# Fewer warm-up matmuls, an earlier load of the beta row, and x matmuls moved ahead of kv groups at the start of an attention and SwiGLU-like kernel

## The chip, the cores and the metric

One core of one Trainium2 chip. The metric is the device time of one execution in microseconds (us). The kernel before took 282.32 us, median of 3 runs (282.05, 282.32 and 292.75). The span of the profiled execution, 280.1 us, is what the engines show between first and last instruction. "Granted clock" is the mean clock of the TensorE in an execution as the profile records it, 1.0 being full.

## The reference

Shapes: q, k, v are 8 batches x 8 heads x 576 rows x 64. The feed-forward has 512 inputs, 2048 hidden units, 512 outputs, on 4608 rows.

```python
q_s = exp(q - max(q, -1));  q_s = q_s / (sum(q_s, -1) + 1e-9)      # softmax over head_dim
k_s = exp(k - max(k, 2));   k_s = k_s / (sum(k_s, 2) + 1e-9)       # softmax over the rows
kv  = einsum('bhsd,bhse->bhde', k_s, v)
x   = einsum('bhsd,bhde->bhse', q_s, kv)   # heads side by side: 4608 x 512
h   = x @ w_in
out = (h * (1 / (1 + exp(-beta * h)))) @ w_out
```

## The kernel before

The program is scheduled by hand: each engine gets its instructions in the order of the source. Batch 0 begins on empty buffers. Its heads are handled in four pairs ("groups"): q is exponentiated, normalised and transposed (`tpe`), k is exponentiated (`kz_exp`), v cast (`vz_cast`), both multiplied into a small kv matrix (`kvz_mm`), which DVE normalises into `kvp` (`kvz_norm`), and kv times q gives the input of the feed-forward (`xpe`, copied by `xev`). Then `hpe` starts the feed-forward's matmuls.

```python
def warm(n, tag):                       # matmuls on zeros, result unused
    t = ps.tile([P, 512], F32, tag=bank(tag), bufs=1, name=...)
    for _ in range(n):
        nc.tensor.matmul(t[:], xT[2][:, 0, 0:P], xT[2][:, 0, :])

def xpe(c, j, tag):
    t = x_ps[c, j] = ps.tile([P, MAIN], F32, tag=bank(tag), bufs=1, name=...)
    nc.tensor.matmul(t[:], kvp[:, c, j, :], qsT[c][:, :, j, :])

def beta_pe(tag):                       # beta's row turned onto partitions
    tb = ps.tile([P, 512], F32, tag=bank(tag), bufs=1, name="tb")
    nc.tensor.transpose(tb[:, 0 : NJ // 2], beta_r[:, 0 : 2 * P : 2], ident8[:])
    nc.tensor.transpose(tb[:, NJ // 2 : NJ], beta_r[:, 1 : 2 * P : 2], ident8[:])
# ... (cut: the other helpers)
load_q(0, 4, [0]); load_q(0, 4, [1, 2, 3], nc.scalar)
load_kv(k_st, k, 0, "k_st", whole=True)
# v groups 0, 1, 2; beta row; v group 3; then w_in block 0 in four, w_in block 1 in two, w_out, ...
# ... (cut: memsets)
warm(18, tag="b0")
# ... (cut: exps and sums of q)
warm(10, tag="acc2")
tpe(0, 2, "acc3")
# ... warm(1), tpe(0, 1), warm(1)
kvz_mm(0, 0, "acc3", 1)                 # kv 0
tpe(0, 3, "acc1")
kvz_mm(0, 1, "acc2", 1)                 # kv 1
beta_pe("acc0")
kvz_mm(0, 2, "acc3", 1)                 # kv 2
xpe(0, 0, "acc1")                       # x 0
kvz_mm(0, 3, "acc2", 1)                 # kv 3
xpe(0, 1, "acc0"); xpe(0, 2, "b3")      # x 1, x 2
hpe(0, 0, [0], "b0"); hpe(0, 1, [0], "b1")
xpe(0, 3, "acc3")                       # x 3
# ... (cut: the rest; the calls for ACT, DVE and POOL stand between these lines)
```

The softmax here doesn't subtract the row's maximum and nothing guards it: scores larger than these inputs give would overflow.

## Time and profile before

| | before |
|---|---|
| median of 3 runs | 282.32 us |
| span of the profile | 280.1 us |
| TensorE (PE) busy | 275.6 us, 98% |
| first v group landed | 10.11 us |
| kv 1 begins | 12.21 us |
| h matmuls without large gaps from | 15.17 us |
| first matmul into the output accumulators | 21.89 us |

The lines behind this table are in the prediction. To read them: an engine's row lists start, length, engine, source line, operation, output and input, and in square brackets how long the engine was idle just before and what ended that. PEld is the loading of weights, which runs beside PE; ACT, DVE and POOL are the scalar, vector and GpSimd engines, SP the one that issues most transfers. A matmul's printed length is its modelled end (0.38 us); in a dense stream of 512 columns one starts every 0.217 us.

### The profile page before, as it was taken

To read this page: it belongs to the slowest core of one execution; us is meant where nothing else is said; L and a number is where in the kernel's file an instruction comes from. 1 tells how busy PE (TensorE), PEld (TensorE's weight loads), DVE (VectorE), ACT (ScalarE), POOL (GpSimd) and SP (SyncE) were. 2 spreads that over 40 slices of the span, in tenths; PEclk is the share of its full clock that TensorE was granted. 3 is DMA by queue.
4 is the path that set the end of the run, shared out by engine and by line. 5 is a ranking of instruction groups with operands and counts; after the bars stand their busy time and mean duration, and the time that the engine had idled before them with its cause. 6 is when DMAs were issued, how large, how long until landed. Compare 5 with 4: busy or idle time off the path is not lost.

```text
span 280.1 us, 4485 instructions
## 1 busy us (share of the span) xinstructions
PE 275.6 (98%) x1744; PEld 128.7 (46%) x1744; DVE 175.3 (63%) x285; ACT 162.6 (58%) x248; POOL 38.3 (14%) x58
## 2 busy tenths in 40 slices
PE   8999999999999999999999999999999999999995
PEld 3544454444444444444444444444444544444544
DVE  3964786994478456945595549553864596354362
ACT  3767885948486447744684559444733574454451
POOL 1555237133030003000300030000000000000000
DMA  7999999999981992199418951641144034005004
GB/s 247 391 378 392 386 389 324 315 278 154 320 284 43 252 289 75 71 237 278 125 78 218 274 147 75 132 95 75 75 86 142 0 152 75 0 0 152 0 0 150
DMA packets 55316, 50.09 MB, mean 179 GB/s; under 512 B 26616, under 2 KB 47488, under 8 KB 55296
## 3 DMA queue, kind: packets, MB, share of 16 engines
q1 hardware_dynamic: 54368, 48.97, 60.4%
q10 hardware_dynamic: 928, 0.85, 0.9%
q8 instruction: 13, 0.21, 0.3%
q14 instruction: 7, 0.06, 0.1%
HBM read 36.71 MB, written 9.44 MB: 165 GB/s over the span
## 4 chain that ended last, share of the span: by engine, by line
PE 95%; DMA 3%; POOL 1%; SPq 0%; issue 0%; ACT 0%
PE h L404 44%; PE acc L453 44%; DMA v_st<-in_v_dram 3%; PE kv L342 2%; PE x L373 1%; PE acc L445 1%; PE kv L317 1%; PE x L389 1%; POOL va L174 1%; PE tp L298 0%; SPq L132 0%; SPq L109 0%; ACT o L172 0%; PE x L364 0%; PE tb L565 0%
## 5 line engine op out<-in xcount | busy, mean ns | idle before, releaser
L418 DVE SCALAR_TENSOR_TENSOR g<-th,h 128x512 bf16<-128x512 bf16 x144 | 96.2, 682 | 79.3 <-ACT th L414 79.0
L414 ACT ACTIVATE th<-h,beta_t 128x512 bf16<-128x512 f32 x144 | 97.8, 686 | 81.0 <-PE h L404 80.3
L404 PE MATMUL h<-xT,w_in_b 128*128 128x512 bf16 x576 | 143.2, 379 | 0.0
L453 PE MATMUL acc<-w_out_b,g 128*128 128x512 bf16 x560 | 141.0, 379 | 0.0
L404 PEld LDWEIGHTS <-w_in_b 128*128 128x128 bf16 x576 | 55.9, 98 | 66.3 <-ACT w_in_b L172 0.7
L453 PEld LDWEIGHTS <-g 128*128 128x128 bf16 x560 | 53.8, 98 | 66.0 <-issue 2.5
L174 POOL CAST va<-v_st 128x2048 bf16<-128x2048 f32 (+2 forms) x14 | 17.1, 1231 | 115.7 <-DMA v_st<-in_v_dram 115.7
L262 DVE TENSOR_REDUCE rq<-eq 128x16 f32<-128x1024 bf16 (+1 forms) x20 | 22.1, 1105 | 5.7 <-ACT eq L251 5.3
L268 DVE TENSOR_TENSOR eq<-eq,rq 128x1024 bf16<-128x1024 bf16 (+1 forms) x20 | 22.9, 1151 | 0.1
L172 ACT CAST xT<-x 128x512 bf16<-128x512 f32 x18 | 9.9, 588 | 17.0 <-PE x L373 14.9
L251 ACT ACTIVATE eq<-q_st 128x1024 bf16<-128x1024 f32 (+1 forms) x18 | 16.9, 955 | 3.5 <-DMA q_st<-in_q_dram 3.5
L174 DVE COPY o<-acc 128x512 f32<-128x512 f32 (+2 forms) x20 | 12.6, 642 | 3.6 <-PE acc L453 3.4
L172 ACT COPY o<-acc 128x512 f32<-128x512 f32 (+1 forms) x18 | 9.5, 570 | 8.4 <-PE acc L453 4.6
L174 DVE CAST xT<-x 128x512 bf16<-128x512 f32 x18 | 11.5, 683 | 2.6 <-PE x L373 1.8
L193 ACT ACTIVATE ek<-k_st 128x1024 bf16<-128x1024 f32 x12 | 12.6, 1051 | 0.0
L532 PE MATMUL warm<-xT 128*128 128x512 bf16 x30 | 9.4, 469 | 1.2 <-DVE xT L613 1.2
L174 POOL CAST w_in_b<-w_in 128x512 bf16<-128x512 f32 (+1 forms) x9 | 5.9, 660 | 6.1 <-DMA w_in<-in_moe_w_in_dram 6.0
L174 POOL CAST w_out_b<-w_out 128x1024 bf16<-128x1024 f32 x5 | 5.2, 1041 | 6.3 <-DMA w_out<-in_moe_w_out_dram 6.3
L532 PEld LDWEIGHTS <-xT 128*128 128x128 bf16 x30 | 3.4, 117 | 5.7 <-issue 3.0
L186 ACT ACTIVATE ek<-k_st 128x576 bf16<-128x576 f32 x8 | 5.0, 674 | 1.2 <-DMA k_st<-in_k_dram 1.0
L263 DVE RECIPROCAL rq<-rq 128x16 f32<-128x16 f32 (+1 forms) x20 | 4.9, 243 | 0.7
L342 PEld LDWEIGHTS <-ek 128*64 128x64 bf16 x192 | 4.1, 111 | 2.5 <-issue 2.5
(48 smaller groups left out, 83.7 us busy)
## 6 DMA issues: line engine op xcount, KB each, us to landing
out_dram<-o SPq DMA_DIRECT2D x14, 512.0 KB, 3.4
q_st<-in_q_dram SPq DMA_DIRECT2D x25, 256.0 KB, 4.3
k_st<-in_k_dram SPq DMA_DIRECT2D x6, 1024.0 KB, 9.7
v_st<-in_v_dram SPq DMA_DIRECT2D x6, 1024.0 KB, 11.7
w_in<-in_moe_w_in_dram SPq DMA_DIRECT2D x6, 512.0 KB, 9.8
v_st<-in_v_dram SPq DMA_DIRECT2D x8, 288.0 KB, 8.6
w_out<-in_moe_w_out_dram SPq DMA_DIRECT2D x4, 512.0 KB, 9.0
w_out<-in_moe_w_out_dram SPq DMA_DIRECT2D x2, 1024.0 KB, 9.8
```

The source lines that it names most:

```text
L172: eng.copy(dst, src)
L174: eng.tensor_copy(dst, src)
L193: nc.scalar.activation(ek[b][:, :, h, :].rearrange("p i h d -> p h i d"), k_st[b][:, h, 0 : R * D].rearrange("p h (i d) -> p h i d", i=R), ...
L251: nc.scalar.activation(eq[b][:, :, s * m : (s + 1) * m, :].rearrange("p i h d -> p h i d"), q_st[b][:, s * m : (s + 1) * m, :].rearrange(" ...
L262: nc.vector.tensor_reduce(rq[b][:, 0, :, h], eq[b][:, :, h, :], axis=AX.X, op=ALU.add)
L268: eng.tensor_tensor(eq[b][:, :, h, :], eq[b][:, :, h, :], rq[b][:, 1, :, h].unsqueeze(3).to_broadcast((P, R, m, D)), ALU.mult,)
L342: nc.tensor.matmul(t[r * D : (r + 1) * D, j, :], ek[b][:, i, hd, :] if i < R else ekt[(b // 2) % 2][:, ds(hd * D, D)], va[b][:, i, hd, :] ...
L404: nc.tensor.matmul(h[:], w_unit(j, kt), x_of(c)[:, kt, :], start=(kt == 0), stop=(kt == KT - 1),)
L414: nc.scalar.activation(th[:], h_of[c, j][:], ACTF.Tanh, scale=beta_t[:, j : j + 1])
L418: nc.vector.scalar_tensor_tensor(out=g[:], in0=th_of.pop((c, j))[:], scalar=1.0, in1=h_of[c, j][:], op0=ALU.add, op1=ALU.mult)
L453: nc.tensor.matmul(acc[st][:], g[:, ds(st * P, P)], w_out_b[:, j, :], start=(j == 0), stop=(j == NJ - 1),)
L532: nc.tensor.matmul(t[:], xT[2][:, 0, 0:P], xT[2][:, 0, :])
```

## The change

Its intent: less PE time spent on warm-ups that may hold the first transposes; the beta transposes out of the path behind kv 1; x groups as early as their kv is normalised.

```diff
     load_kv(k_st, k, 0, "k_st", whole=True)
+    nc.sync.dma_start(beta_r[:], moe_beta.rearrange("(hh q) -> hh q", q=2 * P))
     load_kv(v_st, v, 0, "v_st", [0])
     load_kv(v_st, v, 0, "v_st", [1])
     load_kv(v_st, v, 0, "v_st", [2])
-    nc.sync.dma_start(beta_r[:], moe_beta.rearrange("(hh q) -> hh q", q=2 * P))
 (cut)
-    warm(18, tag="b0")
+    warm(14, tag="b0")
 (cut)
-    warm(10, tag="acc2")
+    warm(8, tag="acc2")
 (cut)
-    warm(1, tag="acc1")
+    beta_pe("acc0")
     kvz_mm(0, 0, "acc3", 1)
 (cut)
-    beta_pe("acc0")
     kvz_norm(0, 1)
+    xpe(0, 0, "b3")
     kvz_mm(0, 2, "acc3", 1)
 (cut)
-    xpe(0, 0, "acc1")
     kvz_norm(0, 2)
+    xpe(0, 1, "acc0")
     kvz_mm(0, 3, "acc2", 1)
 (cut)
-    xpe(0, 1, "acc0")
     kvz_norm(0, 3)
-    xpe(0, 2, "b3")
+    xpe(0, 2, "acc1")
```

## The prediction

> **What bounds the kernel now.** I read the page first, for the engine that is full and the chain that ends last.
>
> ```profile
> PE 275.6 (98%) x1744; PEld 128.7 (46%) x1744; DVE 175.3 (63%) x285; ACT 162.6 (58%) x248; POOL 38.3 (14%) x58
> ...
> PE   8999999999999999999999999999999999999995
> ...
> DMA  7999999999981992199418951641144034005004
> ...
> PE 95%; DMA 3%; POOL 1%; SPq 0%; issue 0%; ACT 0%
> ```
>
> The TensorE (PE) is the bound for 265 of 280.1 us. Only the first slices are not yet so: the second row begins with 8, and the DMA row is full for the first twelve slices. All parts of the change lie in the first 15 us, so the question is how much earlier, if at all, the dense matmuls can begin. Next came the chain of waits in the window from 0 to 18 us (start, length, what):
>
> ```profile
> 1.74 8.37 DMA v_st<-in_v_dram
> 10.11 0.06 issue
> 10.16 2.00 POOL va L174 x2
> 12.16 0.04 issue
> 12.21 0.48 PE kv L317 x18
> 12.68 0.21 PE tb L565
> 12.89 0.12 PE tb L566
> 13.02 0.41 PE kv L317 x18
> 13.42 0.32 PE x L389
> 13.74 0.41 PE kv L317 x18
> 14.15 0.54 PE x L389 x2
> ```
>
> Up to 12.21 the first v group's landing and two POOL casts set the time, not PE. From there PE works without a gap worth naming. The beta transposes (tb) take 0.33 us there, between kv 1 and kv 2, and one x matmul between two kv groups takes 0.32. Then I read the timeline by engine, in narrow stretches, for what lets each later instruction go:
>
> ```profile
> 13.78 0.58 ACT L172 CAST xT<-x 128x512 bf16<-128x512 f32 x1 [0.56 <-PE x L389]
> 14.51 0.58 ACT L172 CAST xT<-x 128x512 bf16<-128x512 f32 x1
> 14.99 0.62 ACT L172 CAST w_in_b<-w_in 128x512 bf16<-128x512 f32 x1
> 14.90 0.10 PEld L389 LDWEIGHTS <-kvp 128*128 128x128 bf16 x1 [0.28 <-DVE kvp L332]
> 15.66 0.12 PEld L404 LDWEIGHTS <-w_in_b 128*128 128x128 bf16 x2 [0.39 <-ACT w_in_b L172]
> 19.01 0.62 ACT L172 CAST w_in_b<-w_in 128x512 bf16<-128x512 f32 x1
> 19.05 0.61 POOL L174 CAST w_in_b<-w_in 128x512 bf16<-128x512 f32 x1 [0.75 <-DMA w_in<-in_moe_w_in_dram]
> 19.68 0.14 PEld L404 LDWEIGHTS <-w_in_b 128*128 128x128 bf16 x2 [0.29 <-ACT w_in_b L172]
> ```
>
> The last three rows are the ones to see. The second half of w_in block 1 (issued 11.62, 7.4 us to landing) lands at 19.0; its ACT cast ends at 19.63; the weight load that needs it goes at 19.68. From 15.17 to 19.73 PE starts a matmul every 0.217 us and loses 0.23 us in two places: 0.065 at 15.67 (that ACT cast of block 0) and 0.165 at 19.30 (a PSUM bank that the DVE product frees at 19.25). So even with the whole front earlier, the matmul at 19.73 cannot go before about 19.68. That is an anchor set by DMA.
>
> Third, who fills the DMA: over the stretch from 2 to 21 us the windows give a DMA share of 0.83 to 1.10 in every microsecond, 251 to 420 GB/s. There is no empty slot for an earlier issue to fill.
>
> **What the Trainium skill says.** "TensorE: Matmul & The Clock Gate", Part 1, holds that the array runs at 1.2 GHz until about 3.4 us of activity in a free-running window, that it goes back after an idle window of that length, and gives 426.7 and 215.7 ns per 512-column matmul. The trace agrees with the first half: the warm-up weight loads lie 0.43 us apart from 1.59 to 5.81, then matmuls start every 0.217 us. The granted clock column shows 1.00 there too, so it does not show this gate; the spacing does. No fall back is seen. Part 4 adds that transposes do not count as busy in the same way; this trace cannot test it. "DMA: Bandwidth & Descriptors", "Queues, rings and completion order", says that each SDMA engine consumes one issuer's descriptors in ring order. The trace agrees: the four v groups, issued at 1.74 to 3.75, land 8.4 to 8.8 us later, behind k, which lands at 9.3. "SBUF — State Buffer" has a shared DVE and POOL port held for a whole instruction; here the same 128x576 POOL cast took 0.92, 1.13 and 0.66 us, the longest beside a DVE product, which fits. The change does not move those two against each other.
>
> **The change part by part.**
>
> Fewer warm-ups, 18 to 14. Eleven run cold (1.19 + 11 x 0.43 = 5.9); the four removed are fast ones, 4 x 0.217 = 0.87 us. The first transpose moves from 7.32 to about 6.5 (its DVE product ends at 6.30). It gains nothing: its copy on ACT waits in order behind the exps, until 7.81, and after that copy ACT waits for k (1.02 us idle until 9.40). Second group, 10 to 8: 2 x 0.217 = 0.43 us. The next transpose waits at 10.07 for its DVE product (9.31 + 0.64 = 9.95). The eight end about 8.45 instead of 9.7, so PE idles 1.6 us instead of 0.37. Value on the path: 0.
>
> Beta. The row's load is 8 KB and costs SP 0.38 us to issue. Moved ahead of v, it makes v groups 0 to 2 issue 0.42 us later, but their descriptors queue behind k until about 9.3 us, so landing moves only by the 8 KB: at 390 GB/s 0.02 us, on the engines that carry it perhaps 0.04 (an estimate). Beta lands right after k, near 9.4. Its two transposes take the place of the single warm-up before kv 0 (0.31 us), around 10.9, and cost 0.33: nothing, as kv 0 waits for the POOL cast until 11.1. It takes 0.33 us out of the stretch behind kv 1.
>
> x groups earlier. x 0 needs its kvp normalised (DVE 12.30 + 0.23 = 12.53), so it fits straight after kv 1 at 12.62 and fills 0.32, exactly the slot beta left. kv 2 stays at 12.95 (its POOL cast ends 12.76). x 1 now stands before kv 3 and needs the norm of kv 1, which ends at 13.39: it goes at 13.45 rather than 13.36. So kv 3 starts at 13.76 instead of 13.67, and everything behind it in the DVE chain (norm of kv 3, x 3) shifts by +0.09: x 3 at 15.05. Before it, one x matmul fewer lies behind kv 3 (0.22 us), but x 3 already waited 0.28 us for DVE, so that only widens the wait.
>
> What is won: ACT can copy x 0 at 13.23 instead of 13.78 and x 1 at 13.87 instead of 14.51, and ends the w_in cast at 15.10 instead of 15.61. The 0.065 us stall at 15.67 goes.
>
> Sum: +0.09 (x 1 waits for its norm) + 0.04 (8 KB ahead of v) - 0.065 (stall gone) = +0.07 us at 15.7. At 19.73 it is held by the anchor from below (gain at most 0.05), and by carried shift from above. Behind that all is the same work. So the net is -0.05 to +0.1 us on 282.32; I put 282.3.
>
> **The rivals.**
>
> The clock gate falls back. With 8 warm-ups PE is idle from 8.45 to 10.07 and then does only small pieces until 14.4. Within 8.45 to 11.86, work is about 1.4 us (three transposes, one warm-up, beta, one kv), 41% of a window, against some 70% in the sparsest window before. The page names an idle window, and this one is not idle, so I give it 8%. If it happens, the matmuls from about 12 to 18.5 run at 0.43: the 15 in front of 18.5 cost some 3 us more, plus the small pieces; 1.5 to 3.5 us net, 284 to 286. Still within 2%.
>
> The front was late in some runs. The gate's window is free-running, so in an unlucky run 18 warm-ups stay cold to 8.9 and the ten behind them end at 11, holding the transpose that is due at 10.07 by 1 us. Then fewer warm-ups give that back: perhaps 0.5 us after the anchor. For it: this is what trimming is for. Against: the median and the profile of before agree within 0.4 us. Time then: 281.8.
>
> The earlier w_in issues feed DMA better. Semaphores of eight transfers are reused in turn, so the fourth w_in load waits for beta rather than v 0, the fifth for v 0 rather than v 1: 0.7 us earlier at issue. If the queue ran short this would move the anchor; but the share is 1.0 throughout, though the rate dips to 307 GB/s at 14 to 16 us. If it does help: 0.2 to 0.4 us, 282.0.
>
> **Range and chances.** Spread of normal runs 282.05 to 282.32, profile 281.92. Working gives 282.3; the two favourable rivals reach 281.6, and the low clock reaches above 283. Range 281.6 to 283.1. One run in three of before took 292.75; if two of the new ones do, the median leaves the range, so slower is not nil. To be 2% faster, 5.6 us would have to come out of 15 us that DMA sets: chance 0.01. Within 2%: 0.96. Slower: 0.03.
>
> **What would show it.** Right: x 0 at about 12.65, x 1 13.45, kv 3 13.76, x 3 at 15.05, both ACT copies of x half a microsecond earlier, no wait at 15.67, and a weight load waiting for the w_in cast at 19.65 to 19.8. Wrong: h matmuls 0.43 us apart behind 12 us (clock gate); a wait of beta's transposes for DMA; kv 0 later than 11.25; w_in of block 1 landing well before 19.0; or a difference that arises behind 20 us, where no instruction of the change stands.

## The result, and the profile after

The changed kernel took 282.32 us, median of 6 runs (281.72 to 282.88), beside 282.06 for the kernel before, median of 6. The ratio is 1.0009, 95% interval 0.9989 to 1.0030: the same. A ratio is the mean time of one kernel's fast runs over that of the other's in the same rounds, so not quite the ratio of these medians. The prediction said 282.3, range 281.6 to 283.1.

The page of the changed kernel, its rows for busy time, PE and DMA by slice:

```profile
PE 274.5 (98%) x1737; PEld 128.2 (46%) x1737; DVE 175.1 (63%) x285; ACT 162.5 (58%) x248; POOL 38.9 (14%) x58
...
PE   8899999999999999999999999999999999999995
...
DMA  7999999999971893199319941641144034005004
```

PE has 1.1 us less to do, the removed warm-ups (6 + 1), and a second slice below 90%. The span is 279.9 instead of 280.1. The chain of waits of the changed kernel in the window from 0 to 18 us (start, length, what):

```profile
1.74 0.46 SPq L578
...
2.25 7.56 DMA v_st<-in_v_dram
...
9.87 2.13 POOL va L174 x2
...
12.04 0.48 PE kv L317 x18
12.52 0.32 PE x L389
12.84 0.41 PE kv L317 x18
...
13.27 0.39 PE x L389
13.66 0.41 PE kv L317 x18
14.07 0.33 PE x L389
...
14.85 0.37 PE x L389
```

The chain is the old one: v's landing, two POOL casts, kv 1, then alternating kv and x. Beta's load (L578) now stands in it at 1.74 because v's issue follows it, but v landed 7.56 us after its issue instead of 8.37, at 9.81 instead of 10.11: the later issue cost nothing. The earlier landing is not a benefit of the change: k landed earlier too, and the first v cast begins 0.79 us after the first exp of k, against 0.76 in before and 0.80 in its repeat. So I compare from the start of kv 1:

| start, us after kv 1 | before | predicted | after |
|---|---|---|---|
| x 0 | 1.15 | 0.44 | 0.41 |
| x 1 | 1.87 | 1.24 | 1.23 |
| kv 3 | 1.46 | 1.55 | 1.55 |
| x 3 | 2.75 | 2.84 | 2.79 |
| first matmul into the accumulators | 9.68 | | 9.65 |

Starts come from the timeline of PE (kv 1 at 12.21 and 12.04). The predicted column takes the prediction's x 0 at 12.65, x 1 at 13.45, kv 3 at 13.76 and x 3 at 15.05, minus 12.21. Each instruction lies within 0.05 us of its place. Then the timeline of the changed kernel by engine, for the waits that the prediction named:

```profile
12.88 0.59 ACT L172 CAST xT<-x 128x512 bf16<-128x512 f32 x1
13.70 0.59 ACT L172 CAST xT<-x 128x512 bf16<-128x512 f32 x1 [0.23 <-PE x L389]
14.18 0.62 ACT L172 CAST w_in_b<-w_in 128x512 bf16<-128x512 f32 x1
14.83 0.10 PEld L389 LDWEIGHTS <-kvp 128*128 128x128 bf16 x1 [0.49 <-DVE kvp L332]
18.73 0.61 POOL L174 CAST w_in_b<-w_in 128x512 bf16<-128x512 f32 x1 [1.38 <-DMA w_in<-in_moe_w_in_dram]
19.45 0.10 PEld L404 LDWEIGHTS <-w_in_b 128*128 128x128 bf16 x1 [0.24 <-ACT w_in_b L172]
```

Counted from kv 1, ACT copies x 0 0.73 and x 1 0.64 us earlier than before (0.55 and 0.64 were written), the stall of 0.065 us behind the first w_in cast is gone, and x 3 only waits longer for DVE (0.49 instead of 0.28 us), as written. From the first accumulator matmul to the end there are 258.2 us in both profiles (280.1 - 21.89 and 279.9 - 21.69): nothing arises later.

One thing in the result was not in the working's centre. The six runs lie on two levels: 281.72, 281.82, 281.94 at a mean granted clock of 0.999 to 1.000, and 282.70, 282.82, 282.88 at 0.994. The experiments are about these levels first.

### The profile page after: what moved, and what is told of

Read it like the earlier page. It is cut to its first block, busy times and chain, and to the rows that moved or that the text cites. A ratio compares the mean times of both kernels' runs of the same rounds, so it can differ in the third digit from the quotient of the medians.

```text
span 279.9 us, 4471 instructions
## 1 busy us (share of the span) xinstructions
PE 274.5 (98%) x1737; PEld 128.2 (46%) x1737; DVE 175.1 (63%) x285; ACT 162.5 (58%) x248; POOL 38.9 (14%) x58
## 4 chain that ended last, share of the span: by engine, by line
PE 95%; DMA 3%; POOL 1%; SPq 0%; issue 0%; ACT 0%
PE h L404 44%; PE acc L453 44%; DMA v_st<-in_v_dram 3%; PE kv L342 2%; PE x L373 1%; PE acc L445 1%; PE kv L317 1%; PE x L389 1%; POOL va L174 1%; PE tp L298 0%; SPq L578 0%; SPq L132 0%; SPq L109 0%; ACT o L172 0%; PE x L364 0%
## 5 line engine op out<-in xcount | busy, mean ns | idle before, releaser
L532 PE MATMUL warm<-xT 128*128 128x512 bf16 x23 | 7.9, 507 | 1.2 <-DVE xT L613 1.2
L354 DVE RECIPROCAL rk<-kv 128x4 f32<-128x4 f32 x6 | 1.1, 182 | 6.5 <-PE kv L342 6.5
```

## The experiments

Twelve measurements of nine kernels, each on one chip and beside runs of the kernel before. All gave correct results, and each was within 2% of before. Theory A: the shorter warm-up lets the TensorE's clock fall back for a while in part of the runs. Against it stand chance by chip, and the parts of the change that are no warm-ups.

**again_before**, the kernel before, unedited.

> The kernel before against itself, to read the mean granted clock of each of its runs, which the first measurement of it did not list. What is to be explained: three of the six runs of the changed kernel took 281.7 to 281.9 us at a mean clock of 0.999 to 1.000, the other three 282.7 to 282.9 us at 0.994. Theory A (the shorter warm-up lets the clock gate fall back for one window of about 3.4 us in part of the runs: 0.5 x 3.4 / 280 = 0.006 of the mean clock): here all runs show 0.999 or more, and 281.8 to 282.4 us. Theory B (the two levels are a property of the chip or of its start, not of the change): here too some of the runs show 0.994 and lie about 1 us higher.

Measured: 281.73 to 282.33, clocks 0.998 to 1.000, median 282.15; ratio 0.9999. 38 runs of before list their clock: 281.55 to 282.46, none below 0.998, mean 282.04. So the lower level of the clock is not the chip's. The runs of before are not all alike either. In the profile of this repeat the matmul spacing changes from 0.43 to 0.217 us only at about 7.1 us, after 14 matmuls, against 11 in the first profile. I had taken the transposes at 10.40, right behind the warm-ups, for a hold. The DVE timeline says no: the next DVE copy goes at 10.83, at once behind a product, and kv 1 at 12.47 behind a POOL cast that had begun late. In this profile the warm-ups cost nothing.

**again_after**, the changed kernel, unedited.

> The changed kernel again, on the same chip. Theory A and theory B both: two levels, 281.8 and 282.8, the upper one at a clock of 0.994, in roughly half of the runs; if the profiled run falls into the upper one, its matmuls are 0.43 us apart over some 3.4 us between 8 and 19 us. Theory C (the two levels were a matter of that chip's DMA): no run at 0.994, all within 0.4 us.

Measured: five runs at 281.76 to 282.05 (clock 0.998 to 1.000) and one at 282.71 (0.994). Ratio 0.9997 (0.9984 to 1.0010). The second level is back, which speaks against theory C, but in one run of six and not in half (the record does not name the chip of the first result). The profiled run was not in it. Its kv 1 begins at 12.38 and its first accumulator matmul at 22.03, again 9.65 us later.

**warm_only**, only the warm-up groups cut.

```diff
-    warm(18, tag="b0")
+    warm(14, tag="b0")
-    warm(10, tag="acc2")
+    warm(8, tag="acc2")
```

> The kernel before with only the two warm-up groups cut (18 to 14, 10 to 8); beta's load and transposes and the order of x and kv groups stay. Theory A: the two levels of the changed kernel come back, part of the runs at 0.994 and about 1 us higher. Theory A2 (it is the single warm-up that beta's transposes replaced, or the moved x groups, that starves the gate): one level, 281.8 to 282.4, clock 0.999 or more.

Measured: 281.70 to 282.11, no run at 0.994, ratio 0.9994 (0.9982 to 1.0006). That is what A2 says, though five runs cannot exclude a share of a quarter: at 4 in 17, the share found in all in the end, five runs without a low one come up one time in four. Its profile shows something else:

```profile
19.25 0.62 ACT L172 CAST w_in_b<-w_in 128x512 bf16<-128x512 f32 x1 [0.16 <-DMA w_in<-in_moe_w_in_dram]
19.92 0.11 PEld L404 LDWEIGHTS <-w_in_b 128*128 128x128 bf16 x2 [0.51 <-ACT w_in_b L172]
```

Here w_in block 1 landed at 19.2, and the weight load waited 0.51 us for its cast. The first accumulator matmul came 9.87 us after kv 1, 0.2 more than in before. This is the anchor of the prediction at work: its landing differs by half a microsecond between runs (18.7 to 19.2 in these profiles).

**warm_back**, the changed kernel with the old warm-ups.

```diff
-    warm(14, tag="b0")
+    warm(18, tag="b0")
-    warm(8, tag="acc2")
+    warm(10, tag="acc2")
```

> The changed kernel with the warm-up groups of before (18 and 10), beta and x moved as in the change. Theory A: one level, no run at 0.994; median 281.8 to 282.3, that is within 0.2 us of before, since beta and the x groups lie on slack (my working: plus 0.05 to plus 0.1). If beta and x were worth something of their own, this kernel shows it without the clock: below before by more than 0.3 us.

Measured: 281.70 to 282.35, median 281.98, ratio 0.9997 (0.9985 to 1.0009), clocks 0.999 or more. First accumulator matmul 9.65 us after kv 1, as in the changed kernel, 0.03 less than in before. So beta and the x groups are worth about 0.03 us on the path, within the -0.05 to +0.1 of the working. None of the five runs fell; that they never make the clock fall by themselves is not shown by so few.

**gap_wide**, the second group cut further.

```diff
-    warm(8, tag="acc2")
+    warm(2, tag="acc2")
```

> The changed kernel with only 2 instead of 8 warm-ups in the second group, so that PE stands still from about 7.2 to 10 us. So far 4 of 13 runs of the changed kernel, none of the 17 runs of before whose clock is listed, and none of 5 each of the two halves had a mean clock of 0.994 and 282.7 us or more. Theory A (the sparse stretch ahead of 14 us makes the clock gate fall back for one window, when the window lies badly): most of the runs, at least 4 of 6, at 0.994 or less and 282.7 us or more; a profile in that state shows matmuls 0.43 us apart somewhere between 9 and 19 us. Theory D (the fall back has nothing to do with warm-ups, chance by chip): at most 2 of 6.

Measured: all six runs low. (The expectation's 13 and 17 do not match the record, which then had 12 runs of the changed kernel and 16 of before with a clock.) Two at 282.57 and 282.58 with a clock of 0.994, four at 283.68 to 284.40 with 0.988; ratio 1.0052 (1.0033 to 1.0072). The profile fell at 0.994. Its windows (PE, PEld, DVE, ACT and POOL busy, then granted clock, DMA share and GB/s):

```profile
9.84:11.02 1.18, 1.15 (x11) 0.83 (x11) 1.18 (x3) 1.18 (x3) 1.17 (x2) 1.00 1.05 391
11.02:14.44 3.42, 3.42 (x61) 2.25 (x60) 2.21 (x10) 1.96 (x5) 2.79 (x5) 0.50 1.03 382
14.44:15.99 1.55, 1.33 (x22) 0.69 (x23) 1.20 (x6) 1.10 (x2) 0.90 (x2) 1.00 1.05 396
```

and its timeline of PE:

```profile
11.04 0.71 PE L317 MATMUL kv<-va,ek 64*64 64x65 bf16 x18
11.68 0.61 PE L298 MATMUL tp<-identity,eq 128*128 128x128 bf16 x4
12.21 0.70 PE L317 MATMUL kv<-va,ek 64*64 64x65 bf16 x18
12.85 0.61 PE L389 MATMUL x<-qsT,kvp 128*128 128x512 bf16 x1
13.38 0.71 PE L317 MATMUL kv<-va,ek 64*64 64x65 bf16 x18
...
14.53 0.48 PE L317 MATMUL kv<-va,ek 64*64 64x65 bf16 x18
```

The clock is 0.50 for 3.42 us, and 0.5 x 3.42 / 280 is the 0.006 missing from the mean. A kv group takes 0.64 us from its start to the next instruction instead of 0.41. x 3 comes 3.56 us after kv 1 instead of 2.79, the first accumulator matmul at 22.63, 10.42 after instead of 9.65: 0.77 us. kv 1 itself is late too. The POOL cast that it needs ended at 11.92, but it stands behind the slow transposes of group 3 (the row at 11.68) and goes at 12.21, 2.36 us after the first v cast began, against 2.17 in the changed kernel: 0.19 us more. Together one stretch costs 0.96 us. The run's time, 282.57, is only 0.75 above the 281.82 us that the changed kernel takes at full clock, since v landed early in it (first v cast at 9.85). A clock of 0.988 would be two such stretches; none was profiled. Theory A stands for this kernel, theory D falls.

The same profile hints at why not every run of the changed kernel falls. Its first warm-ups change from 0.43 to 0.22 us apart at about 4.2 us (weight loads at 3.72, 4.15, 4.39, 4.61), which is 2 x 3.42 us ahead of the fall at 11.02. Opening, fall and return thus lie on one grid of 3.42 us, and the stretch of that grid ahead of the fall, 7.60 to 11.02, held 1.15 us of PE work. In the repeat of the changed kernel that kept its clock the spacing changes at about 4.0 us, and the same stretch of its grid, 7.40 to 10.82, held 2.23 us. Two profiles do not make a limit, but where the grid lies differs from run to run.

**gap_filled**, the second group made longer instead.

```diff
-    warm(8, tag="acc2")
+    warm(14, tag="acc2")
```

> The changed kernel with 14 instead of 8 warm-ups in the second group, which fill PE until about 9.8 us when the gate opens early. Theory A: no run at 0.994. In runs in which the gate opens late, the warm-ups hold the transpose that is due at about 10.1 us, as the repeated run of before shows (transpose at 10.40, directly behind them): then 282.2 to 282.5. So 281.8 to 282.5 and a clock of 0.998 or more throughout. Theory D: an 0.994 in some run.

Measured: 281.71 to 282.10, all at 1.000, ratio 0.9996 (0.9983 to 1.0009). No fall, as theory A says; with gap_wide, in which all six fell, the number of warm-ups in this group is the only difference. No run at 282.2 or above either, so the late hold did not show.

**fillers**, three single warm-ups in places where PE waits.

```diff
-    warm(8, tag="acc2")
+    warm(9, tag="acc2")
     tpe(0, 1, "acc2")
 (cut)
+    warm(1, tag="acc1")
     beta_pe("acc0")
 (cut)
     tpe(0, 3, "acc1")
+    warm(1, tag="b0")
```

> A candidate that is to beat both: the changed kernel with a ninth warm-up in the second group and one warm-up each in two places where PE waits anyway, ahead of beta's transposes (about 10.7) and behind the transposes of group 3 (about 11.8, POOL's cast ends about 12.1). Theory A: fewer runs at 0.994 than the changed kernel, best none of 6, and neither late start: median 281.8, against 282.1 of before. If it is no better than the changed kernel in this, a run or two of six lies at 282.7.

Measured: 281.96 to 282.21, median 282.04, clocks 0.999 and 1.000, ratio 1.0001 (0.9989 to 1.0013). No run was low, but five such runs would come up one time in four at a share of 4 in 17, and the median did not reach the 281.8 expected: as a candidate it is a miss. In the profile kv 0 goes at 11.44, behind the pushed-back beta transposes, and kv 1, behind the filler after group 3, at 12.39, 2.40 us after v's first cast began at 9.99. In the changed kernel that is 2.17: the fillers cost 0.23 us on the path, which is what the median lacks (282.04 against 281.82).

**extra_load**, a useless load of 256 KB ahead of w_in block 1, into a tile that nobody reads.

```diff
 (cut: the tile pad is declared)
     w_load("in", 0, 3)
+    nc.sync.dma_start(pad[:], w_out_d[:, 7, 0, :])
     w_load("in", 1, 0)
```

> The changed kernel with a useless load of 256 KB (into a tile of its own that nobody reads) ahead of w_in block 1. My prediction held that the landing of w_in block 1's second half sets the time of one matmul and all that follows. Then 256 KB at about 390 GB/s, 0.67 us, lets that half land 0.67 us later and the matmul that needs it starts 0.5 to 0.65 us later, measured from the start of kv 1: time 282.3 to 282.5 for runs at full clock. Rival (there is slack behind this landing, PE is not bound by it): the matmul waits longer but nothing or less than 0.2 us arrives at the end: 281.8 to 282.0.

Measured: 282.25 to 282.47, median 282.42, ratio 1.0013 (1.0001 to 1.0024). Its mean is 282.39, 0.57 us above the changed kernel at full clock (runs of other calls) and 0.37 above before in its own call. The timeline:

```profile
19.44 0.62 ACT L173 CAST w_in_b<-w_in 128x512 bf16<-128x512 f32 x1 [0.43 <-DMA w_in<-in_moe_w_in_dram]
20.11 0.12 PEld L405 LDWEIGHTS <-w_in_b 128*128 128x128 bf16 x2 [0.54 <-ACT w_in_b L173]
```

The landing moved from about 18.7 to 19.4 and the weight load from 19.45 to 20.11; the first accumulator matmul came 10.13 us after kv 1, 0.48 more. The rival would have had less than 0.2 arrive. A second wait appeared too, for the first half of block 1 at 18.81. So DMA, here the w_in landing, leaves little slack: most of what is put ahead of it arrives at the end.

**hold_more**, the kernel before with four more warm-ups.

```diff
-    warm(18, tag="b0")
+    warm(22, tag="b0")
```

> The kernel before with 22 instead of 18 warm-ups in the first group. In the profile of its repeat the clock gate opened late (14 cold warm-ups) and the ten of the second group ran up to the transpose of group 2, which went at 10.40 at once behind them instead of waiting for DVE. Theory E (warm-ups that run too long hold the transposes and with them kv and all behind; this is what the change was meant to remove): four more cost 0.87 us when fast, 1.7 when cold; the transpose of group 2 goes at 10.4 to 11.5 directly behind the warm-ups, and the time rises to 282.3 to 283.0, in runs with a late gate most. Rival: kv 1 waits for POOL's cast of v until 12.2 anyway, so nothing arrives at the end: 282.0 to 282.2.

Measured: 282.01, 281.87, 282.19, 282.18, 282.60 and 282.89; median 282.18, ratio 1.0013 (0.9999 to 1.0026). The interval still holds 1, and the median lies in the range of the rival (282.0 to 282.2) and under that of theory E; only two of six runs reached the latter. The one profile, of a run at 282.19, does show the mechanism:

```profile
10.65 0.42 DVE L174 COPY qsT<-tp 128x512 bf16<-128x512 bf16 x1 [0.24 <-PE tp L298]
10.99 1.09 DVE L268 TENSOR_TENSOR eq<-eq,rq 128x512 bf16<-128x512 bf16 x1
12.14 0.11 PEld L298 LDWEIGHTS <-eq 128*128 128x128 bf16 x2 [0.55 <-DVE eq L268]
```

The transpose of group 2 goes at 10.23, directly behind the warm-ups, DVE waits 0.24 us for it, and its next product takes 1.09 us instead of 0.76: it now begins just after a POOL cast (10.88) instead of ahead of one. PE then waits 0.55 us for that product, and kv 1 goes at 12.56 though the POOL cast that it needs had ended at 11.55. From the first v cast, at 9.89, that is 2.67 us instead of the 2.16 of the repeat of before. So warm-ups that run to 10.2 us cost 0.5 us in this run, through DVE; its total does not show it because v landed early. That 18 of them do this in the kernel before was in neither of its two profiles.

**third_after** (the changed kernel), **warm_only_2** and **gap_filled_2**, all unedited repeats.

> The changed kernel a third time, for the share of runs in which the gate falls back: so far 4 of 12 at 0.994 and 282.7 to 282.9. Theory A: again about a third, 1 to 3 of 6; the others at 281.7 to 282.1. If none of six, the share is smaller than read so far.

Measured: 281.66 to 281.90, no run at 0.994, ratio 0.9993 (0.9981 to 1.0005). So the share of low runs is smaller than read so far: 4 of 17 in all. By call they came 3 of 6, 1 of 6 and 0 of 5.

> The kernel before with only the two groups cut, again: 0 of 5 at 0.994 so far. It keeps a single warm-up ahead of kv 0, which in the changed kernel beta's transposes replace. If the cut of the groups alone makes the gate fall back, 1 to 3 of 6 here as in the changed kernel; if the removed single warm-up is needed too, none again, and 281.7 to 282.2.

Measured: 281.75 to 282.18, none at 0.994, ratio 0.9999. Ten runs without a fall in all; at a share of 4 in 17 that would happen by chance in 7% of cases.

> The changed kernel with 14 warm-ups in the second group again, the best candidate: no run at 0.994, median 281.9, 0.1 to 0.3 us below before, its interval against before still holding 1.

Measured: 281.54 to 282.11, median 281.95, ratio 0.9997 (0.9985 to 1.0009), no fall. It is not shown to beat before, as the intervals hold 1. In its profile w_in block 1 landed late, at 19.2, as in warm_only, and the first accumulator matmul came 9.91 us after kv 1.

## Why the prediction was right

**What bounds the start.** Right. v's landing, the POOL casts, then PE until the feed-forward. Beta's earlier load did not delay v, and the instructions moved to within 0.05 us of the written places, counted from kv 1.

**Beta and x groups: -0.05 to +0.1 us.** Right: -0.03 in the profiles of the changed kernel, its two repeats and warm_back, where the first accumulator matmul comes 9.65 us after kv 1 against 9.68 in the two of before. In the terms of the sum, x 3 came 0.04 us later rather than 0.09, the stall of 0.065 went, and the 8 KB of beta ahead of v showed no cost.

**The anchor at w_in block 1.** Right in kind, and tested: 0.57 us for 256 KB. It does not hold every run. In warm_only and gap_filled_2 it added 0.2 us, in the profiled changed kernel nothing, since there the landing was early. The prediction read the weight load's wait for the ACT cast as the sign of it, and that is not enough. In gap_wide the half landed at 18.66, ACT began the cast only at 19.71, behind three activations in its order, and the weight load waited the same 0.24 us as in the changed kernel. The landing sets the time where the cast itself waits for DMA, as in the rows of warm_only and extra_load.

**Earlier w_in issues.** This rival gained nothing that shows. The second half of block 1 was issued at 10.58 instead of 11.62 us, and landed 8.86 us after the first v cast began, against 8.89 before.

**The clock gate.** The step that was mis-sized. The prediction gave a fall-back 8% and a cost of 1.5 to 3.5 us, with the clock low from about 12 to 18.5 us. Of the 17 runs of the changed kernel 4 (24%) had the mean clock of one such stretch. They took 282.78 us in the mean, the 13 others 281.82: 0.96 us, two thirds of the least that I gave. The term that was too large is the stretch: 6.5 us written, 3.42 measured. In the one profile of a fall, in gap_wide, it lies from 11.02 to 14.44, over small pieces that partly wait for POOL and DVE anyway, and costs the same 0.96 us; I had put the dense h matmuls behind 15 us into it. No profile of the changed kernel itself fell low, so that its stretch lies there too is taken over from gap_wide. The four runs of gap_wide at 0.988, 1.9 to 2.6 us above 281.82, do reach the cost written. Which part brings it about is not settled: neither the groups' cut alone (0 of 10 runs) nor the missing single warm-up with long groups (warm_back, 0 of 5) did it. All parts together did it in 4 of 17. That is consistent with needing both, but at such counts not shown. That the change does it at all is clear: none of 38 runs of before fell.

**The fronts that were late.** The prediction offered 281.8 if fewer warm-ups give back a hold. At full clock the changed kernel is at 281.82 in the mean, 0.22 us under the 282.04 of 38 runs of before, on pooled chips. The sign fits; the size is under the half microsecond that the prediction gave for a hold. The cause is not shown: hold_more shows that a hold is possible, but neither profile of before has one. Nor can so few profiles find 0.22 us, since the first v cast begins anywhere from 9.85 to 10.31 us in them, whichever the kernel. What remains of the 0.22 us beyond the 0.03 stays open.

**The sum.** 13 runs with 0.22 us won and 4 with 0.74 lost (282.78 - 282.04) come to (4 x 0.74 - 13 x 0.22) / 17 = 0.01 us. So the time stayed where it was. The forecast of 282.3 was right with its centre on slack that cancels; that two larger terms also cancel was luck. One run of before in its first three took 292.75 us; none of the later runs was like it, and its clock is not recorded, so it is left unexplained.

## What to carry to other kernels

Before moving instructions at the start of a kernel, find the landing that the first dense stretch waits for: here a load of 256 KB put ahead of it (0.67 us at 390 GB/s) added 0.57 us at the end, while taking 0.33 us off the path ahead of it came to 0.03. Warm-up matmuls can cost time on both sides, by the work that they hold (hold_more) and, when there are too few, by the sparse stretch in which the clock falls (gap_wide), so measure the granted clock of many runs and not one profile. When runs of one kernel lie on two levels, look at the clock before pooling them: a mean of 282.04 hid 281.82 and 282.78.

## What the Trainium skill lacked or had wrong

- "TensorE: Matmul & The Clock Gate", Part 1, names an idle window as the cause of a fall-back. In gap_wide the clock fell at 11.02 us although PE had been busy for 1.15 us since 9.84 by the profile, and the changed kernel, with six more warm-ups there, fell in 4 of 17 runs. This need not contradict the page: all of the 1.15 us but one warm-up are transposes, which Part 4, as the prediction cites it, does not count as busy in the same way; no run here separates the two. The page gives no share of busy time below which the clock falls. Its window length agrees: 3.42 us at 0.50.
- No page says that a profile's granted clock misses the first cold stretch of an execution. In these runs it reads 1.00 in the first microseconds, where matmuls start 0.43 us apart, and 0.50 in the later fall-back. My prediction took the first for the rule, which was wrong for the second.
- "DMA: Bandwidth & Descriptors" has no spread for a landing in a saturated queue. The same w_in load with the same bytes ahead of it landed at 18.7 to 19.2 us in different runs, enough to move the end by 0.2 us.
